# A transformer block on one core: the last chunk's matmuls in whole-array form, with single-product waits and late evacuations on ScalarE

## Chip, core and metric

The kernel runs on one core of a Trainium2 chip. Five engines work in parallel, each through its own list of instructions: TensorE (PE in the profile; its weight loads are PEld), VectorE (DVE), ScalarE (ACT), GpSimd (POOL) and SyncE (SP, which here only issues DMAs). They are tied together by semaphores. TensorE writes its results into PSUM, eight banks of 512 float32 per partition; VectorE or ScalarE must carry them from there into SBUF ("evacuation")[...]. The metric is the device time of one execution in microseconds; lower is better.

## What is computed

One adaLN-conditioned block over 2048 tokens of width 640: attention with 32 heads of 20, then a gated MLP of width 1536. Everything is bfloat16.

```python
mod = (_silu(c) @ w_mod).reshape(c.shape[0], 6, 1, -1)
sa, ca, ga, sb, cb, gb = ...
h = _layernorm(x) * (1 + ca) + sa
x = x + ga * attention(h)          # wqkv, softmax(q k / sqrt(20)) v, wo
h = _layernorm(x) * (1 + cb) + sb
x = x + gb * (((h @ w_gate) * (h @ w_up)) @ w_down)
```

The gate has no nonlinearity: gate and up products are multiplied element by element.

## The kernel before

**A planner writes the program.** The Python code does not emit instructions in program order. It creates tasks (class `Task`, L31) with an engine, a planned duration in ns, dependencies, a priority and a gate, and a small event simulation (`Sched`, L115, run at L289) decides in which order each engine takes them. That order is then fixed: `emit_program` (L317) writes each engine's list with the semaphore waits that the dependencies need. So the planned durations decide an order, and the chip's own durations decide the time. The planner's constants that matter here are: 136 ns for a matmul of 320 columns (`C320`, L821), n / 2.4 + 3 ns for n columns (`X`, L823), 170 ns until a matmul's result is out (`PE_DRAIN`, L14), 100 ns for a change of TensorE's tiling mode (`PE_SWITCH`, L15), 60 ns for a semaphore (`SEM`, L13), and n x 1.042 + 67 ns for VectorE on n float32 columns from PSUM (`ps_cost`, L482).

**Attention.** The queries go through in five chunks of 512, 512, 512, 256 and 256 tokens (`CHUNKS`, L427), numbered 0 to 4, each in eight sets of four heads. Scores are matmuls with 32 rows of weights (L1292, mode "S"). Most of their exponentials are ScalarE activations over two or three PSUM banks (L1328, into the tile PP); the rest are built on VectorE from integer operations (L1352, L1384, L1389, L1392). The product with the values is L1811 (mode "P", four 128x32 tiles). The order on TensorE is chosen by `pick_pe` (L1959), which puts scores first, then value products, then other matmuls through `pick_x` (L1884).

**Rounds.** All other matmuls are grouped in a `Round` (L786): a list of matmuls that accumulate into one bank, and the evacuation after them. Only the first matmul of a round carries dependencies; the others follow it. A matmul may be given as `quarters` (L815): four instructions, each with 32 of the 128 weight columns, on four column tiles of the array, one bank together. These run in mode "P", a plain matmul in mode "X"; L817 is the line of every quarter.

**Projections and the suffix.** K, Q and V projections of the later head sets are spread over chunk 0's attention (L1230 to L1263). A V round (`v_round`, L1095) covers 128 tokens and half of the 640 columns; there are 32 of them. After a chunk's attention comes its suffix (`suffix`, L1517): the out-projection (two halves of 320 columns per 128 tokens, five matmuls over Ocp and one over OcT), its evacuation with the residual (L1561), LayerNorm statistics on VectorE (L1571, L1573, L1574), a power on GpSimd (L1576), the normalisation into xn2 (L1578), transposes (L1589), their evacuation into h2T with scale and shift (L1594), twelve gate and twelve up rounds of five matmuls (weights in stx or stg), gate evacuation (L1664, in the last chunk L1666 on ScalarE), the product (L1675) into hprod, then the down-projection: for each 128 tokens two passes of 320 columns and twelve matmuls each (round names dn), evacuated with the residual at L1695, and the output DMA (L1701). VectorE's normalisations and GpSimd's powers share a lock in the planner (L146), so that it does not let them overlap. Tiles of chunk 3 have a t at the end (xckt, hprodt), those of chunk 4 a c.

Chunk 0 to 3's suffixes are spread over the next chunk's attention by gates. Chunk 4's has nothing to hide under. It starts while the end of chunk 3's is still open: its out-projection and its transposes have priority over chunk 3's down passes, its gate and up rounds come behind them. In this last stretch the five banks of the attention join the two or three that rounds use.

**Stealing.** Some evacuations (`evac`, L684) carry a second form for ScalarE. Where ScalarE is idle in the plan and VectorE is not free, `steal` (L267) moves such a task over. It does so only up to a plan time of 66.2 us (`STEAL_END`, L25), that is, before the exponentials fill ScalarE.

Of the kernel before, what the change touches and what calls it, by code (L numbers as in the profile page):

```python
# [12 lines left out]
SEM = 60.0  # L13
# [101 lines left out]
class Sched:  # L115

    def __init__(self):
        self.tasks = []
        self.order = {k: [] for k in ("sp", "act", "pe", "dve", "pool")}
        self.all = []  # L120
        self.free_at = {k: T0 for k in self.order}
        self.pend = {k: [] for k in self.order}
        self.readyl = {k: [] for k in self.order}
        self.t = 0.0
        self.n = 0
        self.progress = 0
        self.dma_free = 0.0
        self.pe_mode = None
        self.pe_end = 0.0
        self.pick_pe = None  # L130
        self.every = []
        self.ham_w = 0
        self.ham_act = 0.0
        self.cold = True
        self.ncold = 0
        self.nfill = 0
        self.ndup = 0
        self.nsteal = 0
        self.nx = 0
        self.hist = []  # L140
        self.acts = []
        self.left = 0
        self.lk_end = {"dve": 0.0, "pool": 0.0}
        self.lk_last = None
# [122 lines left out]
    def steal(self):  # L267
        if self.t > STEAL_END or (self.pend["act"] and self.pend["act"][0][0] < self.t + STEAL_GAP):
            return False
        self.pull("dve")  # L270
        best = None
        for task in self.readyl["dve"]:
            if task.alt is not None and (best is None or (task.prio, task.seq) < (best.prio, best.seq)):
                best = task
        if best is None or self.free_at["dve"] <= self.t and best is min(self.readyl["dve"], key=lambda x: (x.prio, x.seq)):
            return False
        if not self.acquire(best, self.t):
            return False
        self.readyl["dve"].remove(best)
        best.eng = best.ctr = "act"  # L280
        best.dur, f = best.alt
        best.emits = [f]
        best.lat = ACT_LAT
        self.finish_issue(best, self.t, best.dur)
        self.free_at["act"] = self.t + best.dur
        self.nsteal += 1
        return True
# [169 lines left out]
D_RES = 75  # L457
PVMIN, PVMAX, PVCAP = 2, 11, 16
GATE_F = [0.8, 0.869, 0.999, 0.673, 1.0]
FILL_MIN = 4200.0  # L460
# [29 lines left out]
def build_kernel(nc, A_x, A_wqkv, A_wo, B_x, B_w_gate, B_w_up, B_w_down, c, w_mod, out):  # L490
# [295 lines left out]
    class Round:  # L786
        def __init__(self, mms, deps, after, prio, gate=0, name="", banks=None):
            banks = banks or G
# [10 lines left out]
            for i, (dur, f) in enumerate(mms):  # L799
                t = Task("pe", dur, wrap(f), deps if i == 0 else (), ctr="pex", prio=prio, gate=gate, name=name,  # L800
                         mode="P" if isinstance(f, list) else "X")
                if i > 0:
                    follower[id(self.tasks[-1])] = t
                self.tasks.append(t)
# [7 lines left out]
            self.evac = after(self)  # L812
            self.evac[-1].on_start = lambda task: banks.done(b["b"], task)

    def quarters(n, lhs, rhs, st, sp, c0=0):  # L815
# [278 lines left out]

    def v_round(t, ch, prio, gate=0):  # L1095
        mms = []
        for k in range(KD):
            f = quarters(320, lambda k=k: hT[t // 4][:, k, t % 4 * 128:t % 4 * 128 + 128],
                         lambda k=k: wV[:, k, 320 * ch:320 * ch + 320], k == 0, k == KD - 1)
            mms.append((C320, f))  # L1100

        def after(r):
            f = lambda e: e.tensor_copy(
                Vf[:, (t * H + 16 * ch) * VW:(t * H + 16 * ch + 16) * VW].rearrange("p (h w) -> p h w", w=VW)[:, :, 1:VW],
                ps[:, r.b["b"], 0:320].rearrange("p (h w) -> p h w", w=DH))
            fa = lambda e: e.copy(
                Vf[:, (t * H + 16 * ch) * VW:(t * H + 16 * ch + 16) * VW].rearrange("p (h w) -> p h w", w=VW)[:, :, 1:VW],
                ps[:, r.b["b"], 0:320].rearrange("p (h w) -> p h w", w=DH))
            return [evac(320, ps_cost(320), f, fa, [r.last, p_on])]
        r = Round(mms, list(t_hT[t // 4]) + [d_wv[ch]], after, prio, gate=gate, name=f"V{t}.{ch}")  # L1110
        v_ready[(t, ch)] = r.evac[0]
        proj_last.append(r.last)
        kv_last.append(r.last)
        v_last.append(r.last)
# [49 lines left out]
    while ap < NA:  # L1164
# [4 lines left out]
        glist.append((us, 0 if even else 3))  # L1169
    NG = len(glist)  # L1170
    gstart = []
    for ci in range(NC):
# [69 lines left out]
    for tc in range(4):  # L1242
        for j in range(1, NSET if tc in K_ALL else 0):
            late.append((j + tc / 4 - KD_LEAD, 2560, lambda p, g, j=j, tc=tc: kq_round("K", j, tc, p, g)))
        for b in range(0 if tc in K_ALL else nblk(tc)):
            r0 = b * 128 + k_base(tc)
            j0 = max(0 if tc not in K_DIRECT else 1, -(-(r0 - 91) // 80))
            late.append((j0 + tc / 4 - K_LEAD, 2560, lambda p, g, b=b, tc=tc: packed_round("K", b, tc, p, g)))
    for t in range(NT):
        late.append((4 + t / NT + V_L, 1600, lambda p, g, t=t: v_round(t, 1, p, g)))  # L1250
    ql = [(tc, b) for tc in range(1, 4) for b in range(KD) if tc not in LATEQ]
# [265 lines left out]
    def suffix(ci):  # L1517
# [8 lines left out]
        slot = ci % 2  # L1526
        tail = ci == NC - 1
        t0 = q0 // 128
        gb = int(gstart[ci + 1]) if not tail else 0
# [18 lines left out]
        for tl in range(ntl):  # L1548
            ev = []
            for hf in range(2):  # L1550
                mms = []
                for k in range(KD):
                    f = quarters(320, lambda k=k, tl=tl: Ocp[:, slot, k, tl * 128:(tl + 1) * 128],
                                 lambda k=k, hf=hf: wo_sb[:, k, 320 * hf:320 * hf + 320], k == 0, False)
                    mms.append((C320, f))
                f = quarters(320, lambda tl=tl: OcT[:, oc_last[ci]["s"], tl * 128:(tl + 1) * 128],
                             lambda hf=hf: wo7[:, 320 * hf:320 * hf + 320], False, True)
# [48 lines left out]
        for fc in range(FT):  # L1606
# [21 lines left out]
            if n <= 256 and GU_ONE:  # L1628
                mms = []
                for w_ in range(2):  # L1630
                    for k in range(KD):
                        f = quarters(n, lambda k=k, cell=wbuf[w_]: cell["t"][:, k, :], lambda k=k: h2T[:, k, 0:n],
                                     k == 0, k == KD - 1, w_ * n)
                        mms.append((X(n), f))
# [21 lines left out]
            for w_ in range(2):  # L1656
                mms = []
                for k in range(KD):
                    f = quarters(n, lambda k=k, cell=wbuf[w_]: cell["t"][:, k, :], lambda k=k: h2T[:, k, 0:n],
                                 k == 0, k == KD - 1)  # L1660
# [24 lines left out]
        for tl in range(ntl):  # L1685
            ev = []
            for hf in range(2):
                mms = []
                for fc in range(FT):
                    f = quarters(320, lambda fc=fc, tl=tl: hprod[:, fc, tl * 128:(tl + 1) * 128],  # L1690
                                 lambda fc=fc, hf=hf: wd_sb[:, fc, 320 * hf:320 * hf + 320], fc == 0, fc == FT - 1)
                    mms.append((C320, f))

                def after(r, tl=tl, hf=hf):
                    f = lambda e: e.tensor_tensor(xck[:, tl, 320 * hf:320 * hf + 320], ps[:, r.b["b"], 0:320],  # L1695
                                                  xck[:, tl, 320 * hf:320 * hf + 320], ALU.add)
                    return [dve(ps_cost(320), f, [r.last, t_xn2[tl]], prio=1)]
                r = Round(mms, t_wd + hp, after, pr(), gate=gate(FT * 320), name=f"dn{ci}.{tl}")
                ev.append(r.evac[0])
# [55 lines left out]
    def pv_candidates(t, maxn):  # L1755
# [9 lines left out]
        for u in info["aq"][:maxn]:  # L1765
            if u.task is None or u.task.done + SEM > t:
                break
            if any(v_ready[(kt, u.j // 4)].done is None or v_ready[(kt, u.j // 4)].done + SEM > t for kt in u.kts):
                break
            res.append(("a", u))  # L1770
        for (qi, jj) in info["dq"]:
            st_ = d_state[qi]
            src = st_["src"].get(jj)
            if src is None or any(x.done is None or x.done + SEM > t for x in src):
                continue
            if any(v_ready[(kt, u.j // 4)].done is None or v_ready[(kt, u.j // 4)].done + SEM > t
                   for u in st_["units"] for kt in u.kts):
# [40 lines left out]
    def pv_issue(cands, t):  # L1818
# [6 lines left out]
        for kind, x in cands:  # L1825
            if kind == "a":
# [3 lines left out]
                ems = pv_emit(u, lambda pbuf=pbuf, p=p, off=off: pbuf[:, p, off:off + 512])  # L1830
                deps = [u.task] + [v_ready[(kt, u.j // 4)] for kt in u.kts]
                if not info["started"]:
# [11 lines left out]
            else:  # L1844
                qi, jj = x
                st_ = d_state[qi]
                for xx, u in enumerate(st_["units"]):
                    srcf = lambda s_=st_["ss"][jj], xx=xx: DSS[:, s_, xx * 512:(xx + 1) * 512].bitcast(BF16)
                    ems = pv_emit(u, srcf)
                    deps = list(st_["src"][jj]) + [v_ready[(kt, u.j // 4)] for kt in u.kts]  # L1850
                    if not info["started"]:
# [32 lines left out]
    def pick_x(t, warm=False):  # L1884
# [3 lines left out]
        if xcur[0] is not None:  # L1888
            cand = xcur[0]
        else:  # L1890
            for task in rl:
# [67 lines left out]
    def pick_pe(t):  # L1959
# [87 lines left out]
        if cands:  # L2047
            cands = pv_balance(cands, force)
            nwork = sum(1 if k == "a" else 4 for k, _ in cands)
            if cands and (nwork >= (PVMIN if just_s[0] else PVMAX) or force):  # L2050
                just_s[0] = False
# [4 lines left out]
        if pick_x(t):  # L2056
            return True
        if cands and not js and len(cands) >= 2:
            pv_issue(cands, t)
# [92 lines left out]
```

## Time and profile before

| | |
|---|---|
| five runs | 827.27, 827.59, 828.51, 829.33, 830.47 us; median 828.51 |
| the profiled execution | 827.59 us, of which 825.4 us are the span from the first to the last instruction |
| granted TensorE clock | 0.998 |
| TensorE busy | 795.0 us (96%), 12504 matmuls |
| ScalarE busy | 775.9 us (94%), 820 instructions |
| VectorE busy | 724.0 us (88%), 1272 instructions |
| last exponential ends | 787.4 us |
| last evacuation (L1695) | 822.66 us, 0.49 us long |

A busy share is an average over stages; which stage has which limit is read from the profile's forty slices of about 20.6 us and from the chain of waits, which follows the last instruction back, at each step to what released it. A group of instructions is named by line, engine, operation, output and inputs, then comes the number of them, their busy time in us and the mean of one in ns, and the idle time just before them with the one who ended it. "issue" means that an engine waited for nothing that the profile shows. A matmul's own duration includes its way through the array: one of 320 columns is 0.30 us long, one of 256 columns 0.27, one of 128 columns 0.22; several of them are under way at a time, so what counts in a stream is the distance from start to start.

### The profile page before, as it was taken

How to read it: one execution, taken by the hardware profiler on the slowest of the kernel's cores; microseconds unless marked ns; L12 is line 12 of the kernel's file. 1: busy time of each engine (PE TensorE's matmuls, PEld its weight loads, DVE VectorE, ACT ScalarE, POOL GpSimd, SP SyncE). 2: the span in 40 equal slices, each digit the busy share in tenths (PEclk: the TensorE clock that was granted, in tenths of full speed). 3: DMA queues.
4: the chain of work that ended last, by engine and by line, in shares of the span. 5: the costliest groups of instructions: out<-in, count | busy, mean ns of one | idle time of the engine just before them, and what ended most of it. 6: DMA issues, size and time to landing. Idle time of an engine off the chain costs nothing.

```text
span 825.4 us, 28913 instructions
## 1 busy us (share of the span) xinstructions
PE 795.0 (96%) x12504; PEld 298.3 (36%) x12504; DVE 724.0 (88%) x1272; ACT 775.9 (94%) x820; POOL 71.5 (9%) x104
## 2 busy tenths in 40 slices
PE   7999999999999999999999999999899999998988
PEld 4433233222232222223333222233244344554567
DVE  7878899989899999999999999999689898657763
ACT  5889999999999999999999999999999999999921
POOL 2300000000011000000011000000021000001000
PEclk9999999999999999999999999999999999999999
DMA  9453311124400136100310122000401226106420
GB/s 303 138 141 82 89 38 35 49 67 126 109 14 25 42 73 168 25 6 23 69 33 6 45 54 56 11 23 19 83 4 23 54 69 141 37 30 141 93 69 19
DMA packets 115900, 54.31 MB, mean 66 GB/s; under 512 B 83771, under 2 KB 115775, under 8 KB 115775
## 3 DMA queue, kind: packets, MB, share of 16 engines
q1 hardware_dynamic: 114847, 51.33, 24.4%
q8 instruction: 99, 1.62, 0.8%
q10 hardware_dynamic: 928, 1.15, 0.5%
q14 instruction: 26, 0.21, 0.1%
HBM read 41.75 MB, written 8.41 MB: 61 GB/s over the span
## 4 chain that ended last, share of the span: by engine, by line
PE 60%; ACT 25%; DVE 8%; issue 5%; DMA 2%; SPq 0%; ACTq 0%; DVEq 0%
ACT PP L1328 25%; PE ps_all L817 21%; PE ps_all L1292 20%; PE ps_all L1811 14%; PE ps_all L1023 3%; DVE DB L1352 2%; DVE DSS L1389 1%; PE ps_all L971 1%; DVE DSS L1392 1%; DMA wm<-in_w_mod_dram 1%; PE ps_all L938 1%; DMA stg<-in_B_w_up_dram 1%; DVE DSS L1384 0%; DMA QT<-q_rows 0%; PE ps_all L831 0%
## 5 line engine op out<-in xcount | busy, mean ns | idle before, releaser
L1328 ACT ACTIVATE PP<-ps_all 128x1024 bf16<-128x1024 f32 (+1 forms) x781 | 758.2, 1146 | 6.3 <-PE ps_all L1292 5.0
L1292 PE MATMUL ps_all<-QT,KT 32*128 32x512 bf16 (+1 forms) x2560 | 318.7, 340 | 16.8 <-ACT PP L1328 10.9
L1352 DVE TENSOR_SCALAR DB<-ps_all 128x512 int16<-128x512 f32 x396 | 263.1, 681 | 33.4 <-PE ps_all L1292 31.7
L1292 PEld LDWEIGHTS ps_all<-QT,KT 32*128 32x128 bf16 x2560 | 85.1, 91 | 285.7 <-ACT PP L1328 243.6
L1811 PE MATMUL ps_all<-PP,Vf 128*32 128x512 bf16 (+2 forms) x2084 | 163.1, 343 | 0.0
L1389 DVE TENSOR_TENSOR DSS<-DB,DSS 128x2048 bf16<-128x2048 bf16 x99 | 122.1, 1233 | 0.0
L817 PE MATMUL ps_all<-h2T,stg 128*32 128x512 bf16 x1440 | 114.7, 382 | 0.8 <-DVE DB L1352 0.5
L1477 POOL TENSOR_TENSOR OTn<-OT,invT 128x512 bf16<-128x512 f32 (+1 forms) x39 | 40.2, 1030 | 603.6 <-DVE invT L1475 596.9
L1811 PE MATMUL ps_all<-DSS,Vf 128*32 128x512 bf16 (+3 forms) x952 | 77.7, 348 | 0.6 <-DVE DSS L1392 0.2
L1811 PEld LDWEIGHTS ps_all<-PP,Vf 128*32 128x32 bf16 (+1 forms) x2084 | 46.5, 94 | 87.6 <-issue 81.7
L1392 DVE TENSOR_SCALAR DSS<-DB 128x2048 int16<-128x2048 int16 x99 | 69.0, 697 | 0.0
L1384 DVE TENSOR_SCALAR DSS<-DB 128x2048 int16<-128x2048 int16 x99 | 67.2, 679 | 0.6
L817 PE MATMUL ps_all<-wd,hprod 128*32 128x320 bf16 x1152 | 57.9, 301 | 0.2 <-DVE DB L1352 0.2
L817 PEld LDWEIGHTS ps_all<-h2T,stg 128*32 128x32 bf16 x1440 | 31.4, 95 | 30.8 <-issue 17.7
L1664 DVE CAST gsb<-ps_all 128x512 bf16<-128x512 f32 (+1 forms) x48 | 29.4, 613 | 7.1 <-PE ps_all L817 6.8
L817 PE MATMUL ps_all<-wo,Ocp 128*32 128x320 bf16 x640 | 34.1, 301 | 0.7 <-DVE DB L1352 0.4
L817 PEld LDWEIGHTS ps_all<-wd,hprod 128*32 128x32 bf16 x1152 | 27.6, 96 | 17.0 <-issue 8.7
L1811 PEld LDWEIGHTS ps_all<-DSS,Vf 128*32 128x32 bf16 (+1 forms) x952 | 24.0, 95 | 24.3 <-issue 13.3
L1023 PE MATMUL ps_all<-hT,wq 128*32 128x512 bf16 x375 | 31.3, 382 | 0.3 <-DVE DB L1352 0.2
L817 PE MATMUL ps_all<-wV,hT 128*32 128x320 bf16 x640 | 30.6, 301 | 0.2 <-DVE hT L946 0.2
L1472 DVE STREAM_TRANSPOSE OT<-ps_all 128x512 f32<-128x512 f32 (+1 forms) x40 | 24.2, 604 | 3.8 <-PE ps_all L1811 3.6
L1675 DVE TENSOR_TENSOR hprod<-ps_all,gsb 128x512 bf16<-128x512 f32 x36 | 24.5, 681 | 3.0 <-PE ps_all L817 2.8
(119 smaller groups left out, 517.1 us busy)
## 6 DMA issues: line engine op xcount, KB each, us to landing
stg<-in_B_w_gate_dram SPq DMA_DIRECT2D x50, 160.0 KB, 4.8
stg<-in_B_w_up_dram SPq DMA_DIRECT2D x50, 160.0 KB, 4.3
QT<-q_rows SPq DMA_DIRECT2D x22, 128.0 KB, 3.1
KT<-k_rows SPq DMA_DIRECT2D x84, 32.0 KB, 1.8
wm<-in_w_mod_dram SPq DMA_DIRECT2D x3, 800.0 KB
x<-in_A_x_dram SPq DMA_DIRECT2D x7, 320.0 KB
xck<-in_A_x_dram SPq DMA_DIRECT2D x3, 640.0 KB, 4.2
wd<-in_B_w_down_dram SPq DMA_DIRECT2D x1, 1920.0 KB
```

Source lines behind the costliest of these rows:

```text
L817: return lambda e, b: e.matmul(ps[32 * x:32 * x + 32, b, c0:c0 + n], lhs()[:, 32 * x:32 * x + 32], rhs(), tile_position=(0, 32 * x), start ...
L1023: f = [lambda e, b_, k=k, x=x: e.matmul(ps[x:x + min(32, w - x), b_, :], wx[:, k, r0 + x:r0 + min(x + 32, w)], hT[tc][:, k, :], tile_posit ...
L1292: ems.append(lambda e, i=i, kt=kt: e.matmul(dstf()[:, i * u.n:(i + 1) * u.n], KT[32 * u.s:32 * u.s + 32, u.j, kt * 128:(kt + 1) * 128], QT ...
L1328: return e.activation(PPs[g % 2][:, cellp["p"], 0:nu * 512], ps[:, b0:b0 + nu, :].rearrange("p b c -> p (b c)"), AFT.Exp, scale=ESCALE)
L1352: return e.tensor_scalar(DB0[:, st_["slot"], x * 512:(x + 1) * 512], bank(cell["b"]), EBIAS, 0.0, op0=ALU.add, op1=ALU.max)
L1384: return e.tensor_scalar(DSS[:, st_["ss"][0], :], DB0[:, st_["slot"], :], 0x7F, 0x3F00, op0=ALU.bitwise_and, op1=ALU.bitwise_or)
L1389: return e.tensor_tensor(d, DB0[:, st_["slot"], :].bitcast(BF16), d, ALU.mult)
L1392: return e.tensor_scalar(DSS[:, st_["ss"][1], :], DB0[:, st_["slot"], :], 0x7F80, 2, op0=ALU.bitwise_and, op1=ALU.bitwise_or)
L1477: f3 = lambda e: e.tensor_tensor(OTn[:, 0:n].rearrange("p (b c) -> p b c", c=32), OT[:, 0:n].rearrange("p (b c) -> p b c", c=32), invT[:, ...
L1664: f = lambda e: e.tensor_copy(gsb[:, gs, 0:n], ps[:, r.b["b"], 0:n])
L1675: f = lambda e: e.tensor_tensor(hprod[:, fc, 0:n], ps[:, r.b["b"], 0:n], gsb[:, gs, 0:n], ALU.mult)
L1811: ems.append(lambda e, i=i, kt=kt, stt=stt, stp=stp: e.matmul(ps[32 * s:32 * s + mc, BPV, 0:u.n], Vf[:, (kt * H + 4 * u.j + s) * VW:(kt * ...
```

## The change

In the last chunk's suffix (`tail`, chunk 4) the new helper `full` takes the place of `quarters` for the out-projection, for gate and up, and for the down-projection: one matmul of 128 weight columns instead of four of 32, in mode "X" instead of "P". The transposes were in mode "X" already. The last of the four down passes is cut in two of 160 columns, each with its own evacuation. The down passes of this chunk no longer carry all twelve products as dependencies of their first matmul: the first ten products stay there, the last two become dependencies of the pass's 11th and 12th matmul (`pdeps`), and `pick_x` gets a check that a following matmul's dependencies are met. `steal` is open again once the last exponential has been started in the plan; of chunk 4's evacuations only those into h2T (L1594) carry a form for ScalarE besides those that were on it already.

```diff
     def steal(self):
-        if self.t > STEAL_END or (self.pend["act"] and ...):
+        if (self.t > STEAL_END and (not TAILX or self.progress < self.ng)) or (self.pend["act"] and ...):
             return False
...
+TAILX = 1
...
-                t = Task("pe", dur, wrap(f), deps if i == 0 else (), ctr="pex", ...
+                t = Task("pe", dur, wrap(f), deps if i == 0 else pdeps.get(i, ()), ctr="pex", ...
...
+    def full(n, lhs, rhs, st, sp, c0=0):
+        return lambda e, b: e.matmul(ps[:, b, c0:c0 + n], lhs(), rhs(), start=st, stop=sp)
...
+        qf = full if tail and TAILX else quarters
...
-            for hf in range(2):
+            cuts = [(0, 320), (320, 320)]
+            if tail and TAILX and tl == ntl - 1:
+                cuts = [(0, 320), (320, 160), (480, 160)]
+            for (c_, w) in cuts:
                 mms = []
                 for fc in range(FT):
-                    f = quarters(320, lambda fc=fc, tl=tl: hprod[:, fc, tl * 128:(tl + 1) * 128],
-                                 lambda fc=fc, hf=hf: wd_sb[:, fc, 320 * hf:320 * hf + 320], fc == 0, fc == FT - 1)
-                    mms.append((C320, f))
+                    f = qf(w, lambda fc=fc, tl=tl: hprod[:, fc, tl * 128:(tl + 1) * 128],
+                           lambda fc=fc, c_=c_, w=w: wd_sb[:, fc, c_:c_ + w], fc == 0, fc == FT - 1)
+                    mms.append((C320 if w == 320 else X(w), f))
...
+                late_hp = {}
+                if tail and TAILX:
+                    late_hp = {FT - 2: hp[-2:-1], FT - 1: hp[-1:]}
+                r = Round(mms, t_wd + (hp[:-2] if late_hp else hp), after, pr(), gate=gate(FT * w), name=f"dn{ci}.{tl}",
+                          pdeps=late_hp)
...
         if xcur[0] is not None:
             cand = xcur[0]
+            if any(d.done is None or d.done + SEM > t for d in cand.deps):
+                return False
```

The diff also rewrites the V rounds so that the columns can be cut in other parts. The parts set are the two old halves, but the planned duration of a V matmul is now `X(320)`, 136.33 ns, where it was `C320`, 136.0 ns. A further knob (`PV0`) is set to 0, which leaves its conditions as they were.

```diff
+V_PARTS = ((0, 4), (4, 8))
...
-    def v_round(t, ch, prio, gate=0):
+    def v_round(t, pt, prio, gate=0):
+        a, z = V_PARTS[pt]
+        nh = 4 * (z - a)
+        w = nh * DH
...
-            mms.append((C320, f))
+            mms.append((X(w), f))
```

## The prediction, made before the changed kernel was run

> **What bounds the kernel now.** I read three views in this order: the busy tenths (which engine owns which stretch), the costliest groups (does that engine ever wait there), and the chain of waits of the last 38 us (what the end consists of). First the tenths and two groups of the page:
>
> ```profile
> PE   7999999999999999999999999999899999998988
> ACT  5889999999999999999999999999999999999921
> ...
> L1328 ACT ACTIVATE PP<-ps_all 128x1024 bf16<-128x1024 f32 (+1 forms) x781 | 758.2, 1146 | 6.3 <-PE ps_all L1292 5.0
> ```
>
> From slice 4 to slice 38 ScalarE is full: 781 exponentials, and only 6.3 us of waiting ahead of them in the whole run. Nothing can shorten that stretch but those microseconds. The last exponential ends at 787.4; then ScalarE is nearly empty, and 38 us belong to TensorE and VectorE. The chain of waits (start, length, what) from there:
>
> ```profile
> 789.37 9.99 PE ps_all L817 x288
> 799.36 0.02 issue
> 799.39 0.49 DVE xckt L1695
> 799.88 1.61 DVE h2Tc L1594 x5
> 801.48 0.04 issue
> 801.53 13.22 PE ps_all L817 x472
> 814.75 0.22 issue
> 814.97 0.43 PE ps_all L817 x8
> 815.40 0.02 issue
> 815.42 0.44 DVE hprodc L1675
> 815.86 0.04 issue
> 815.90 6.73 PE ps_all L817 x192
> 822.64 0.02 issue
> 822.66 0.49 DVE xckc L1695
> ```
>
> Four TensorE blocks: (1) 789.37 to 799.36, chunk 3's down-projection (four passes of 12 quartets) with chunk 4's out-projection (24 quartets) between its passes; (2) the h2T transposes and a VectorE wait; (3) 801.53 to 815.40, chunk 4's gate and up, 120 quartets; (4) 815.90 to 822.64, its down-projection, 48 quartets. Three holes are worth taking: 1.53 us before 801.53, 0.22 at 814.75, 0.53 before 815.90.
>
> **Part 1: whole-array matmuls.** 24 + 120 + 48 quartets (four 128x32 tiles each) become as many single matmuls. The streaming time does not change: VectorE picks up gate/up products every 1.09 us, ten quartets, so 109 ns per 256-column quartet; block 4's evacuations start 1.63 us apart, 136 ns per 320-column quartet. Four tiles together already stream as fast as one array can. What the change risks is the weight load. These are the tail's only whole-array matmuls before the change (timeline, TensorE and its loads):
>
> ```profile
> 799.26 0.56 PEld L1589 LDWEIGHTS ps_all<-ident,xn2c 128*128 128x128 bf16 x10 [0.27 <-issue]
> 799.26 0.73 PE L1589 MATMUL ps_all<-ident,xn2c 128*128 128x128 bf16 x10
> ```
>
> One such matmul lasts 0.22, so ten start (0.73 - 0.22) / 9 = 57 ns apart, each with a 128-column load of its own. The Trainium skill ("TensorE: Matmul & The Clock Gate", Part 3, "What overlaps and what doesn't") says that a weight load overlaps running matmuls only where the row groups differ; here every load uses all rows, and by the page's load rule (columns / 1.2, 107 ns) 204 loads would add an estimated 21.8 us. By the row the load is hidden even at 57 ns, and the new pitches (109, 136, and 69 by the same scale for 160 columns) are longer. I take the row: **0 us**, and keep the rule as a small chance.
>
> Instruction count falls to a quarter. Block 3 ought to last 119 x 0.109 + 0.27 = 13.24; it takes 13.87, for TensorE twice starts late with no releaser (0.16 before the loads at 811.08, 0.50 before those at 814.97, both "issue"; 0.56 of it shows in the spacing of the products). Bounds: 0 if these stay, -0.56 if fewer instructions remove them. I take **-0.5**.
>
> **Part 2: mode changes and the order they bring.** The out-projection becomes whole-array between passes that stay in quarters. A change costs 0.10: block 1's 72 quartets would let the next matmul start at 789.37 + 72 x 0.136 = 799.16, the transposes start at 799.26. Two more lie on TensorE's full path: +0.2. But the kernel's order is made by its planner, which charges 100 ns for a change too. I follow its constants by hand for the order alone. From the end of the out-projection (0): the last half's evacuation waits for statistics of the half before and ends at 900; statistics 1000 to 1400, aggregate to 1615, epsilon to 1790; the first tile's normalisation to 2150 holds the lock shared with GpSimd; GpSimd's power to 2720; the second tile's normalisation 2840 to 3200; transposes ready at 3300. VectorE's order in the trace is just this one. The second down pass after the out-projection ends at 2 x 1632 = 3264: the transposes miss it by 36 ns, and a third pass goes first, as the trace shows. With two changes it ends at 3364, and the transposes come **before the last pass** by 64 ns. On the chip the operands are there: the second normalisation ended at 797.50, some 0.1 later now, and the pass ends its issue at 797.73.
>
> TensorE then runs from 789.37 without a hole: 72 x 0.136 = 9.79, ten transposes 0.57, five changes 0.5; gate/up start at 800.23 instead of 801.53: **-1.3**. The h2T evacuations lie under the last pass.
>
> **Part 3: late evacuations on ScalarE.** While VectorE evacuates a down pass, the planner hands ScalarE h2T blocks 0, 2 and 4 at a planned 273 ns. The price on the chip, from these groups of the whole run:
>
> ```profile
> L1666 ACT CAST gsb<-ps_all 128x256 bf16<-128x256 f32 x12 | 4.5, 373 | 23.0 <-PE ps_all L817 23.0
> ...
> L944 ACT ACTIVATE hT<-ps_all,mcol 128x512 bf16<-128x512 bf16 x3 | 2.4, 799 | 3.8 <-PE ps_all L938 3.7
> L981 ACT CAST KT<-ps_all 128x512 bf16<-128x512 f32 x3 | 1.8, 587 | 1.2 <-PE ps_all L971 1.2
> ```
>
> 256 columns fewer are 587 - 373 = 214 ns less, so this operation at 256 is near 0.59. Three are 1.8 from about 798.15: done at 799.95, 0.3 before TensorE wants them. **0 us** while the last pass covers them (VectorE alone, 5 x 0.335 after its evacuation, would be as late). Without that cover they would run from 799.55 to 801.35: only 0.13 better than now. No table load shows between L1328 and L944.
>
> **Part 4: down passes wait for single products.** Now the first pass waits for product 11: last up matmul ends 815.40, pass starts 815.90. After, its first ten matmuls need products 0 to 9, the last of which VectorE finished two rounds ago; it starts one pitch (0.11) after the last up matmul's start (815.40 - 0.27), at 815.24: **-0.66**. The new waits stand before its 11th and 12th matmul. Behind them on TensorE are only the rest of this pass and three more; the 12th comes 11 x 0.136 = 1.5 after the first, and product 11 takes 0.6. They never bind. Should the product be 1 us late, that is the most that they can give back.
>
> **Part 5: last half split in two.** 24 matmuls at 69 instead of 12 at 136: +0.03. Evacuation of 160 columns instead of 320: L1695 has 0.49 at 320, L1675 0.43 at 256, so about 0.34: -0.15. Net **-0.12**; the output DMA after it is the same.
>
> **Part 6: what hides in the value projection.** Its parts equal the old halves, and the new PV knob is 0, so both are inert. But the planner's charge per V matmul goes from 136 to 136.33 ns: 32 rounds x 5 x 0.33 = 53 ns of plan time, enough to flip near ties from 17 us on. The chip's work stays the same; its order may not. Bounds: below, all of ScalarE's waiting between 70 and 786 us, 2.9 us; above, the longest stall of an exponential that an order makes in this trace (timeline at 48.5):
>
> ```profile
> 48.53 1.94 ACT L1328 ACTIVATE PP<-ps_all 128x1024 bf16<-128x1024 f32 x2 [2.64 <-PE ps_all L1292]
> ```
>
> There 7 V quartets stood before scores that wait for a K block. I take **0** and keep -2.9 and +2.6 for the range.
>
> **Sum** against the profiled execution (827.59, span 825.4): -0.5 - 1.3 - 0.66 - 0.12 = -2.6, so 825.0. That execution lies 0.9 under the median of 828.51, so the forecast is **825.9**; its own range, 824.7 to 827.1, is the stalls left (+0.56) and some of the plan's scatter.
>
> **Rivals.** (a) *Transposes stay behind the last pass* (the plan's margin is 64 ns): +0.2 for changes, -0.13 for ScalarE, and -0.5 - 0.66 - 0.12 give -1.2: 827.3. For it: the margin; against: the hand sum met the trace's order. (b) *One re-dealt stall* of 2.6 in the attention eats the gain: 828.5. (c) *Slower*: the re-dealt order stalls the exponentials in the projection backlog, 20 to 66 us, where ScalarE is busy 17.9 and 17.4 of 20 us and V, K and scores compete. At 2.64 a stall, two give -2.6 + 5.3 = +2.7: 831.2; it decides once ScalarE's waiting grows by more than 2.6 + 1.7 = 4.3 us. For it: only 2.9 us of waiting in 716 us, hard to keep by chance; against: priorities and gates, which the 53 ns don't touch. (d) *Exposed weight loads*: 825.9 + 21.8 = 847.7; against it the 57 ns.
>
> **Chances.** 0.2% (1.7 us) is about what can be told from no change. Forecast 0.50 (0.44 faster, 0.06 within); (a) 0.16 (0.06 faster, 0.10 within); (b) 0.12 (0.11 within, 0.01 slower); (c) 0.18 slower; (d) 0.02 slower; the attention's order luckier still 0.02 faster. Together 0.52, 0.27, 0.21. The range, 823.6 to 830.9, leaves out most of (c) and all of (d).
>
> **What would show it.** Transposes ahead of the last xckt pass and under 0.3 us of hole before gate/up (part 2); block 3 near 13.3 (part 1); no hole before the down-projection (part 4); a last evacuation near 0.34 (part 5); the last exponential ending within 1 us of 787.4 (part 6). An end of the exponentials at 790 or later, or a pitch over 0.15 in block 3, would make the prediction wrong.

## The result, and the profile after

The changed kernel takes 826.1 us (median of 27 runs) against 828.64 (48 runs of the kernel before), a ratio of 0.9967 with a 95% interval of 0.9959 to 0.9975: 2.1 to 3.4 us faster. The forecast was 825.9.

First the same three lines of the page as before, now of the changed kernel (code lines have moved: L1341 is the exponential, L826 a quarter, L822 a whole-array matmul of the last chunk):

```profile
PE   8999999999999999999999999999898999999998
ACT  5889999999999999999999999999999999999931
...
L1341 ACT ACTIVATE PP<-ps_all 128x1024 bf16<-128x1024 f32 (+1 forms) x781 | 757.8, 1144 | 6.6 <-PE ps_all L1305 5.4
```

The long stretch is as it was: 781 exponentials, ScalarE full, 6.6 us of waiting instead of 6.3. From the start of the first exponential to the end of the last it is 768.84 us, before 768.77. TensorE's last slices have filled. The chain of waits (start, length, what) shows with what:

```profile
790.36 1.81 PE ps_all L826 x48
792.17 3.37 PE ps_all L822 x24
795.54 3.37 PE ps_all L826 x96
798.91 0.67 PE ps_all L1603 x10
799.58 1.75 PE ps_all L826 x48
801.33 19.77 PE ps_all L822 x180
821.10 0.02 issue
821.12 0.33 DVE xckc L1712
```

Read it as one unbroken sequence of work on TensorE: a down pass of chunk 3 (48 quarters), the out-projection (24 matmuls), two more passes, the transposes (L1603), **then** the fourth pass, and 180 matmuls of gate, up and three of the four down passes with the two half passes, without a hole. The transposes have moved ahead of the last pass, and the three holes of before are gone.

A stage by stage account from the two profiles (start of chunk 3's first down pass to the end of the span; each row is a difference of starts and ends in the timeline; a negative entry in the third row means that the first down matmul starts before the last up matmul has ended):

| stage | before | after | difference | foreseen |
|---|---|---|---|---|
| chunk 3's first pass to gate/up | 12.16 | 10.90 | -1.26 | -1.3 |
| gate/up block | 13.84 | 13.27 | -0.57 | -0.5 |
| end of gate/up to the down-projection | +0.53 | -0.16 | -0.69 | -0.66 |
| down-projection to the end of its last evacuation | 7.25 | 7.08 | -0.17 | -0.12 |
| last evacuation to the end | 2.25 | 2.25 | 0 | 0 |
| sum | 36.03 | 33.34 | -2.69 | -2.6 |

The two profiled spans differ by only 1.7 (825.4 and 823.7). The first exponential began 1.26 us later in the profile of after (19.82 instead of 18.56), the exponentials took 0.07 more, and between the last exponential and chunk 3's first down pass 0.34 less went by: 1.26 + 0.07 - 0.34 - 2.69 = -1.70. The late beginning is chance, as the runs below show: over fourteen profiles of twelve different kernels the first exponential began anywhere from 17.24 to 20.60, and the three profiles of the unchanged kernel alone have 18.56, 20.57 and 20.40. So the sections below compare the last stretch (chunk 3's first down pass to the end) of each profile, and take the times of many runs only for the whole. The changed kernel with its two V charges repeats there to some hundredths (33.34 and 33.40, below). The kernel before does not: its three profiles have 36.03, 35.70 and 36.26, so the gain in this stretch is 2.4 to 2.9 us. The experiments on single parts rest on one profile each; by their times, ratios to before of 0.9952 to 0.9978, none of them can be told from the changed kernel.

### The profile page after: what moved, and what is told of

Its sections match the earlier page's. It is cut to its first block, busy times and chain, and to the rows that moved or that the text cites. A ratio compares the mean times of both kernels' runs of the same rounds, so it can differ in the third digit from the quotient of the medians.

```text
span 823.7 us, 27805 instructions
## 1 busy us (share of the span) xinstructions
PE 796.6 (97%) x11952; PEld 297.6 (36%) x11952; DVE 723.9 (88%) x1270; ACT 776.9 (94%) x823; POOL 71.7 (9%) x104
## 4 chain that ended last, share of the span: by engine, by line
PE 61%; ACT 27%; DVE 6%; issue 6%; ACTq 0%; DVEq 0%
ACT PP L1341 27%; PE ps_all L1305 20%; PE ps_all L826 20%; PE ps_all L1831 14%; PE ps_all L822 3%; DVE DB L1365 2%; PE ps_all L980 2%; PE ps_all L1032 1%; DVE DSS L1405 1%; DVE DSS L1402 1%; PE ps_all L947 1%; DVE DSS L1397 0%; PE ps_all L840 0%; PE ps_all L1603 0%; DVE hprod L1689 0%
## 5 line engine op out<-in xcount | busy, mean ns | idle before, releaser
L1341 ACT ACTIVATE PP<-ps_all 128x1024 bf16<-128x1024 f32 (+1 forms) x781 | 757.8, 1144 | 6.6 <-PE ps_all L1305 5.4
L826 PE MATMUL ps_all<-h2T,stg 128*32 128x512 bf16 x1440 | 114.7, 382 | 0.8 <-DVE DB L1365 0.5
L826 PE MATMUL ps_all<-wd,hprod 128*32 128x320 bf16 x1152 | 57.9, 301 | 0.2 <-DVE DB L1365 0.2
L826 PEld LDWEIGHTS ps_all<-h2T,stg 128*32 128x32 bf16 x1440 | 31.4, 95 | 30.8 <-issue 17.7
L826 PEld LDWEIGHTS ps_all<-wd,hprod 128*32 128x32 bf16 x1152 | 27.6, 96 | 17.0 <-issue 8.7
L826 PE MATMUL ps_all<-wV,hT 128*32 128x320 bf16 x640 | 31.5, 301 | 0.2 <-DVE hT L955 0.2
L826 PE MATMUL ps_all<-wo,Ocp 128*32 128x320 bf16 x560 | 30.8, 301 | 0.7 <-DVE DB L1365 0.4
L2102 PE MATMUL ps_all<-ident 128*32 128x512 bf16 x316 | 27.2, 383 | 0.6 <-DVE h2Tt L1608 0.4
L1497 DVE STREAM_TRANSPOSE OcT<-OTn 128x512 bf16<-128x512 bf16 (+1 forms) x40 | 23.9, 597 | 4.4 <-POOL OTn L1490 4.1
```

The lines of the kernel that those rows point to most:

```text
L826: return lambda e, b: e.matmul(ps[32 * x:32 * x + 32, b, c0:c0 + n], lhs()[:, 32 * x:32 * x + 32], rhs(), tile_position=(0, 32 * x), start ...
L1341: return e.activation(PPs[g % 2][:, cellp["p"], 0:nu * 512], ps[:, b0:b0 + nu, :].rearrange("p b c -> p (b c)"), AFT.Exp, scale=ESCALE)
L2102: task.emits = [lambda e, x=x: e.matmul(ps[32 * x:32 * x + 32, b_, :].rearrange("p (a b) -> p a b", a=4), ident[:, 32 * x:32 * x + 32], id ...
```

## The experiments

**The re-dealt order of the attention.** Two kernels separate the planner's new charge for V matmuls from the rest. The first is the changed kernel with the old charge:

```diff
-            mms.append((X(w), f))
+            mms.append((C320, f))
```

> The changed kernel with the planner's charge for a V matmul put back to 136.0 ns, so that the attention is planned as before the change. My theory: the gain lies in the last stretch alone (from the start of chunk 3's first down pass to the end of the span 33.3 us as in the changed kernel, 36.0 before it) and the re-dealt order of the attention is worth nothing, so this kernel is as fast as the changed one, ratio to before 0.9967 +- 0.0010, with first to last exponential at 768.8 us. Rival: part of the gain comes from the luckier order; then the ratio is 0.9980 or more. Opposite rival: the new order costs, and this kernel reaches 0.9955 or less.

Measured: ratio 0.9960 (0.9946 to 0.9974), exponentials 769.30 us from first to last, last stretch 33.40 us. The gain is there in full without the new order of the attention. The exponentials took 0.5 us longer than expected; the three profiles of the kernel before, which is planned with the same charge, scatter as much (768.77, 769.51, 769.39). The second is the kernel before with the new charge alone (`C320` to `X(320)` in `v_round`):

> The kernel before with only the planner's charge for a V matmul raised to 136.33 ns: the re-dealt attention order alone. My theory: no difference, ratio 1.000 +- 0.001, last stretch 36.0 us, exponentials from first to last 768.8 us. Rival: the new order gains or costs 1 us or more, ratio under 0.9988 or over 1.0012.

Measured: ratio 0.9980 (0.9965 to 0.9994), exponentials 768.52 us, last stretch 35.62 us. The attention is indeed as fast as before, but my "no difference" missed: by its interval this kernel is 0.5 to 2.9 us faster than before. Its profile shows where. The gate/up block takes 13.37 us (13.84 before), though it is in quarters as before, and there is no 0.3 us wait for a w_up load. From the end of the last exponential to the end of the span it needs 37.33, the kernel before 38.07. Both differences lie in places that the edit does not reach; a section below returns to them.

**The place of the transposes.** In the next kernel only the out-projection goes back to quarters, so that the two added mode changes fall away in the plan and on the chip:

```diff
-                    f = qf(320, lambda k=k, tl=tl: Ocp[:, slot, k, tl * 128:(tl + 1) * 128],
+                    f = quarters(320, lambda k=k, tl=tl: Ocp[:, slot, k, tl * 128:(tl + 1) * 128],
...
-                f = qf(320, lambda tl=tl: OcT[:, oc_last[ci]["s"], tl * 128:(tl + 1) * 128],
+                f = quarters(320, lambda tl=tl: OcT[:, oc_last[ci]["s"], tl * 128:(tl + 1) * 128],
```

> The changed kernel with the out-projection of the last chunk back in quarters; all else whole-array. My theory: it was the two added mode changes of 100 planned ns that let the transposes go ahead of chunk 3's last down pass; without them the planner puts them behind it again. TensorE saves two real changes of 0.1 us but waits for h2T: last stretch about 34.1 us (33.34 + 1.3 - 0.2 for the changes - 0.3 for two engines on the evacuations). Rival: the whole-array form itself makes the stretch faster, and the place of the transposes is worth little; then it stays within 0.3 us of 33.34.

In the kernel after, all stays whole-array, and the transposes are put behind the last pass by priority:

```diff
-            r = Round(mms, list(t_xn2), after, pr(True), gate=gate(n), name=f"h2T{ci}.{k}")
+            r = Round(mms, list(t_xn2), after, pr(not tail), gate=gate(n), name=f"h2T{ci}.{k}")
```

> The changed kernel, all matmuls whole-array, but the transposes of the last chunk planned behind chunk 3's last down pass by their priority. My theory: TensorE stands idle for about 1 us between transposes and gate/up while ScalarE and VectorE share the evacuations (three of 0.5 us on ScalarE); last stretch 33.34 + 0.9 = 34.2 us. Rival: with two engines the evacuations are so short that the place of the transposes does not matter, under 33.6 us.

The last stretch is 34.25 us for the first and 34.50 for the second, against 33.34. The timeline of the first (out-projection in quarters), at the transposes, their evacuations and the first gate matmuls:

```profile
799.55 0.73 PE L1603 MATMUL ps_all<-ident,xn2c 128*128 128x128 bf16 x10
...
799.87 1.48 ACT L1610 ACTIVATE h2Tc<-ps_all,mcol 128x256 bf16<-128x256 bf16 x3 [11.92 <-PE ps_all L1603]
800.08 0.72 DVE L1608 TENSOR_SCALAR h2Tc<-ps_all,mcol 128x256 bf16<-128x256 bf16 x2
...
801.41 1.26 PE L822 MATMUL ps_all<-h2Tc,stx 128*128 128x256 bf16 x10 [1.12 <-ACT h2Tc L1610]
```

The transposes now end all four passes, and TensorE stands for 1.12 us until ScalarE's third evacuation is through; with priority in place of quarters it is 1.13. Both stretches lie near their theories (34.1 and 34.2) and clear of the rivals: it is the place of the transposes that is worth about 1 us, not the form of the matmul. The second kernel is 0.25 slower than the first; 0.21 of it lies between chunk 3's first pass and gate/up, where it has two mode changes more. And the first kernel shows that the place followed from the mode changes: with the out-projection in mode "P" the plan falls back to the order of before. The gate/up block was 13.27 and 13.28 us in them, the rest as in the changed kernel.

**Late evacuations.** `steal` is closed again after 66.2 us, all else as changed:

```diff
-        if (self.t > STEAL_END and (not TAILX or self.progress < self.ng)) or (self.pend["act"] and ...):
+        if self.t > STEAL_END or (self.pend["act"] and ...):
```

> The changed kernel without late evacuations on ScalarE: VectorE alone carries h2T. My theory: they lie under chunk 3's last down pass and end at most 0.1 us after it, so the last stretch stays 33.34 us, or 33.5 at most. Rival: the evacuations on ScalarE are what closed the hole; then gate/up start 0.5 us or more later.

Last stretch 33.35 us. Its timeline:

```profile
800.97 1.68 DVE L1608 TENSOR_SCALAR h2Tc<-ps_all,mcol 128x256 bf16<-128x256 bf16 x5
801.10 1.48 PEld L826 LDWEIGHTS ps_all<-wd,hprodt 128*32 128x32 bf16 x48
801.11 1.81 PE L826 MATMUL ps_all<-wd,hprodt 128*32 128x320 bf16 x48
802.85 1.64 PEld L822 LDWEIGHTS ps_all<-h2Tc,stx 128*128 128x128 bf16 x16 [0.26 <-DVE h2Tc L1608]
```

VectorE needs 1.68 us for the five blocks and is done at 802.65, while TensorE works on the last pass from 801.11 to 802.92. The bracket at the gate's weight loads names h2T, yet the loads would have had to wait for the pass in any case: gate/up start 10.90 us after chunk 3's first pass, as with ScalarE's help. So this part of the change gains nothing where it stands. Its cover is the last pass; where the two kernels above took that away, the hole is 1.12 us with ScalarE's help and was 1.53 before without it.

**Single products.** The last chunk's passes wait for all twelve products again:

```diff
-                if tail and TAILX:
+                if tail and not TAILX:
                     late_hp = {FT - 2: hp[-2:-1], FT - 1: hp[-1:]}
```

> The changed kernel with the last chunk's down passes waiting for all twelve products again. My theory: TensorE stands idle between the last up matmul and the first down matmul, and the last stretch is 0.66 us longer: 34.0 us. Rival: only the idle 0.53 us that the trace before shows comes back, 33.87 us, for the overlap of the matmuls is there in both.

Last stretch 34.05 us, 0.71 longer. The chain of waits shows the hole:

```profile
798.82 13.22 PE ps_all L822 x120
812.04 0.02 issue
812.06 0.44 DVE hprodc L1689
812.50 0.05 issue
812.54 6.74 PE ps_all L822 x60
```

From 812.04 to 812.54 TensorE does nothing. That is 0.50 us, and the stretch lost 0.71: without the wait the first down matmul starts under the last up matmul, whose own 0.27 us then cost only one pitch of 0.11. That overlap is another 0.16. So the idle time that a page shows is not all that such a wait costs.

**The late starts in gate/up.** Gate and up go back to quarters in the changed kernel (`qf` to `quarters` in their two-round form):

> The changed kernel with gate and up of the last chunk back in quarters (960 instead of 240 TensorE instructions). My theory: the late starts without a releaser come from the number of instructions and come back: gate/up block 0.4 to 0.6 us longer, last stretch 33.8 us. Rival: quarters stream as well as whole-array matmuls and the late starts before were chance: 33.3 us.

The chain of waits:

```profile
797.25 0.67 PE ps_all L1603 x10
797.92 14.85 PE ps_all L826 x528
812.77 6.67 PE ps_all L822 x60
```

528 quarters run without a hole (the last pass's 48 and 480 of gate/up). The block takes 13.27 us and the last stretch is 33.40, so my theory fell: four times the instructions bring no late start here. It also shows once more that whole-array matmuls stream no slower and no faster than quarters. To see whether the late starts of before were chance, the unchanged kernel was profiled twice more.

> The kernel before, unchanged, profiled a second time, for the late starts without a releaser in the gate/up block (13.84 us there instead of 13.27) and the 0.3 us wait for a w_up load before chunk 3's last products. Theory A: they belong to the kernel's layout of instructions and DMAs and come back at the same places: gate/up 13.7 to 13.9 us. Theory B: they are chance of one execution: 13.3 us, and no such wait.

> The kernel before once more, with the same question: A, gate/up 13.7 to 13.9 us and the wait of 0.3 us for w_up; B, 13.3 us and no wait. If this profile and the one before it differ from each other, it is chance.

The weight loads of TensorE in the first profile, then in the second and in the third:

```profile
811.08 1.42 PEld L817 LDWEIGHTS ps_all<-h2Tc,stx 128*32 128x32 bf16 x53 [0.16 <-issue]
812.41 2.06 PEld L817 LDWEIGHTS ps_all<-h2Tc,stg 128*32 128x32 bf16 x72
814.97 0.12 PEld L817 LDWEIGHTS ps_all<-h2Tc,stg 128*32 128x32 bf16 x8 [0.50 <-issue]
```

```profile
817.40 0.12 PEld L817 LDWEIGHTS ps_all<-h2Tc,stg 128*32 128x32 bf16 x8 [0.26 <-issue]
```

```profile
814.91 1.96 PEld L817 LDWEIGHTS ps_all<-h2Tc,stg 128*32 128x32 bf16 x72
817.69 0.12 PEld L817 LDWEIGHTS ps_all<-h2Tc,stg 128*32 128x32 bf16 x8 [0.81 <-issue]
```

In all three profiles of before, the loads of the very last two quartets of the block come late, by 0.50, 0.26 and 0.81 us, and the block takes 13.84, 13.44 and 14.00. The smaller late start of the first profile (0.16) is in neither of the others. So the place of the large one belongs to that program, and its length is chance. No other kernel of this study has such a row, though the one in which only V was charged anew may keep a tenth: its block takes 13.37, and VectorE picks up the last product 1.17 us after the one before, where the ones before are 1.09 apart.

The first profile holds a trail that no run followed. Its two late starts are 53 + 72 = 125 loads apart. The page's instruction queue brought 1.62 MB in 99 packets:

```profile
q8 instruction: 99, 1.62, 0.8%
```

If all of that is TensorE's 12504 matmuls and as many loads, a packet holds an estimated 253 instructions, or 126 pairs of a load and a matmul. It fits that in gate/up and down of this program packets come 3.75 us apart (812.32 and 816.07), and in the changed kernel 13.6 (802.40 and 816.03). So the late starts may stand where one packet's instructions end. That is not shown, and it would not say why the kernel with as many quarters in gate/up runs through.

The wait for w_up comes and goes too. Before chunk 3's last products it shows in all three profiles of before (0.34, 0.41 and 0.45 us; the row is from the third):

```profile
790.44 0.40 PE L817 MATMUL ps_all<-h2Tt,stg 128*32 128x256 bf16 x8 [0.45 <-DMA stg<-in_B_w_up_dram]
```

The changed kernel and seven of its relatives do not wait there, nor does the kernel before with the new V charge, though the DMA queue's order at that point is the same. But two relatives of the changed kernel do: the one with the transposes behind (0.20) and one of the further steps below (0.28). So this wait is no property of the program before. What sets either of the two is open; the number of instructions alone does not.

**Going on.** The same hole stands before chunk 3's first down pass (0.56 us, waiting for its last product, also in the changed kernel). Three steps build on each other: single-product waits for chunk 3 too, with the order of the tail given by hand (the diffs below do not print the lines that give it); chunk 3's passes whole-array as well; the last output DMA cut in two.

```diff
-                if tail and TAILX:
+                if ci >= NC - 2 and TAILX:
                     late_hp = {FT - 2: hp[-2:-1], FT - 1: hp[-1:]}
```

> A further step: chunk 3's down passes too wait for single products, and the planner is told the order (one pass, out-projection, two passes, transposes, last pass). My theory: the 0.56 us hole before chunk 3's first down pass closes. From the end of the last exponential to the end of the span 35.0 us in the changed kernel, here 34.4. Rival: the out-projection then waits for the last attention item's transposes (OcT) instead, and 0.4 us or more of it comes back as a hole there: 34.8 or more.

```diff
-                    f = qf(w, lambda fc=fc, tl=tl: hprod[:, fc, tl * 128:(tl + 1) * 128],
+                    f = (full if ci >= NC - 2 else quarters)(w, lambda fc=fc, tl=tl: hprod[:, fc, tl * 128:(tl + 1) * 128],
```

> The step before (single-product waits for chunk 3 too, order given) and chunk 3's down passes as whole-array matmuls as well, so that TensorE never changes its mode after the last attention item. My theory: five changes of 0.1 us go, up to 0.1 of it lost to waiting for the normalised rows: from the last exponential's end to the end of the span 34.45 - 0.45 = 34.0 us. Rival: the chain through LayerNorm sets the start of the transposes, and 0.3 us or less is gained.

```diff
-            outs.append(dma("sp", 128 * D * 2, lambda e, tl=tl: e.dma_start(outv[:, t0 + tl, :], xck[:, tl, :]), ev,
-                            prio=1))
+            oc = [(0, D, ev)] if len(cuts) == 2 else [(0, 480, ev[:2]), (480, D, ev[2:])]
+            for (o0, o1, es) in oc:
+                outs.append(dma("sp", 128 * (o1 - o0) * 2, lambda e, tl=tl, o0=o0, o1=o1: e.dma_start(
+                    outv[:, t0 + tl, o0:o1], xck[:, tl, o0:o1]), es, prio=1))
```

> As the one before, and the last output DMA cut in two: 480 columns as soon as their evacuations are done, the last 160 columns after the last evacuation. My theory: the DMA behind the last evacuation moves 40 KB instead of 160 KB and ends 0.2 to 0.4 us sooner: 2.3 us from the last evacuation to the end become 2.0, last exponential to end 33.75. Rival: the time is latency and rows of 320 bytes are slow to write, so nothing is gained or 0.1 us lost.

| kernel | last exponential to end | chunk 3's first pass to end | ratio to before |
|---|---|---|---|
| before | 38.07 | 36.03 | 1 |
| changed | 35.04 | 33.34 | 0.9967 (0.9959 to 0.9975) |
| + single products for chunk 3 | 34.45 | 33.37 | 0.9955 (0.9941 to 0.9969) |
| + its passes whole-array | 34.40 | 33.03 | 0.9958 (0.9945 to 0.9970) |
| + output cut in two | 33.93 | 32.76 | 0.9951 (0.9937 to 0.9964) |

The first step gave 0.59, as I had it. The second gave 0.34 of the 0.45 in the part that it touches, and its profile lost 0.28 again to the w_up wait; by the measure named ahead, 34.40 instead of 34.0, it missed. The remaining tenth is a new wait, in the timeline of that kernel:

```profile
797.57 0.49 DVE L1712 TENSOR_TENSOR xckt<-ps_all,xckt 128x320 bf16<-128x320 f32 x1 [0.26 <-PE ps_all L822]
...
798.11 1.47 PEld L822 LDWEIGHTS ps_all<-wd,hprodt 128*128 128x128 bf16 x12 [0.19 <-DVE xckt L1712]
```

TensorE is now so close behind that, by the bracket, the last pass waits for the evacuation of the pass before it. The third step took the end behind the last evacuation from 2.28 to 2.00 us. Together the three are 1.1 us shorter in the profile than the changed kernel. Their intervals lie wholly below 1, so they are faster than the kernel before; that they are faster than the changed kernel, their times do not show, for the intervals overlap.

## Why the prediction was right

**Whole-array matmuls cost nothing (part 1): right.** The row of the transposes was the right guide and the rule on row groups (the Trainium skill, "TensorE: Matmul & The Clock Gate", Part 3) the wrong one. In the changed kernel's timeline the loads have 128 columns, use all rows, and lie beside the running matmuls:

```profile
801.25 10.81 PEld L822 LDWEIGHTS ps_all<-h2Tc,stx 128*128 128x128 bf16 x100 [0.26 <-issue]
801.26 11.09 PE L822 MATMUL ps_all<-h2Tc,stx 128*128 128x256 bf16 x100
```

One matmul is 0.27 long, so 100 of them start (11.09 - 0.27) / 99 = 0.109 us apart, the pitch of the quartets. The estimated 21.8 us of exposed loads did not appear.

**-0.5 for late starts: right in size, wrong in cause.** The block lost 0.57, but the kernel with quarters back keeps that gain. The step that failed is "if fewer instructions remove them". The late start stood at one place of one program, and every kernel that differed from it was rid of it, or of all but a tenth. That the size came out is luck: against the other two profiles of before the same term would be -0.17 and -0.73.

**Mode changes and order (part 2): right.** The order came out as the hand sum had it, with a margin of 64 planned ns, and the gain in that stage was 1.26 for 1.3 foreseen. On the chip it was close too:

```profile
798.84 0.56 PEld L1603 LDWEIGHTS ps_all<-ident,xn2c 128*128 128x128 bf16 x10 [0.27 <-DVE xn2c L1592]
```

The second normalised tile was ready at 798.58, 0.26 before. The bracket names it, but it cost nothing: the same 0.27 stands before the first loads after other mode changes, where it says "issue", and two passes from 795.47 with one change end at about 798.84 in any case.

**Evacuations on ScalarE (part 3): right.** Nothing gained while covered. An evacuation there lasts 0.565 us (0.59 estimated), but three in a row take 1.48 and not 1.8, because they overlap. So the help without cover was sized too small: 0.41 (1.53 to 1.12) instead of 0.13. Only rival (a) rests on that figure.

**Single products (part 4): right.** 0.69 in the profile, 0.71 by experiment, 0.66 foreseen. **The cut last half (part 5)** brought 0.17 for 0.12; the last evacuation is 0.33 us long, as estimated from the slope of its neighbours.

**The V charge (part 6): right for the attention, incomplete otherwise.** The planned order changed in dozens of places on TensorE and VectorE; ScalarE's order of exponentials did not. Their length is the same within 0.1 us in the two profiles; over all fourteen, with either charge, it lies between 768.5 and 770.1. My sign for this part, a last exponential within 1 us of 787.4, did not come (by the timeline the kernel before has 787.33): it ended at 788.66, for the first had begun 1.26 later, and that scatter made it a poor sign. And the edit was not inert: the kernel with it alone has no w_up wait and at most a tenth of the late start, 0.7 us less in its profile. Whether that is the edit or chance is open for the w_up wait. The w_up wait of before (0.34 us) was in the chain that I read, and I gave it no value in either direction.

So of some 3 us between last exponential and end, about 2.1 come from the edits themselves (1.26 by the order, 0.69 by the waits, 0.17 by the cut), and 0.9 from two waits that the first profile of before happened to have. Against its second and third profiles these two are worth 0.6 and 1.2.

## What to carry to other kernels

When a planner orders the work, follow its own arithmetic around the change: a difference of 36 ns in a plan decided about 1 us on the chip, and it came from a cost (the mode change) that looked like a loss. Before helping a step along with a second engine, look at what already covers it; and price a wait at the head of a matmul stream as idle time plus the overlap that is lost. Profile a program more than once before you call a small unexplained hole chance or a property of the program, and compare stages, not spans, where the start scatters more than the effect.

## What the runs showed of the hardware

A change between column tiles and the whole array costs TensorE 0.10 to 0.12 us (in the changed kernel, from 790.36: 12 quartets at 0.136 end at 791.99, the next matmul starts at 792.10). Four 32-column tiles and one whole-array matmul stream at the same pitch, 109 ns for 256 columns and 136 for 320. The beginning of the kernel scatters by 3.4 us from run to run (first exponential from 17.24 to 20.60), with no clear tie to the granted clock of the first 17 us, which was 0.80 to 1.00. In the three profiles of the kernel before it makes 1.8 to 2.0 of the 2.5 to 2.8 us between their spans.
